# A quarter of the input loaded as fp32 on ScalarE's DMA queue, and the prologue's small work put in another order

## The chip, the cores and the metric

The kernel runs on one core of one Trainium2 chip. The metric is the device time of one execution, in microseconds. Three timed runs of the kernel before stand beside one profiled execution, from which every row in this document comes. TensorE appears in the rows as PE (its weight loads as PEld), VectorE as DVE, ScalarE as ACT, GpSimd as POOL and SyncE as SP.

## What is computed

A filter in the frequency domain along the sequence, and then a two-layer network whose activation is a PReLU:

```
X = np.fft.rfft(x, axis=1)                       # x: 8 x 3008 x 256, fp32
Y = X * (filt_r + 1j * filt_i)[None]             # 1505 frequencies x 256
y = np.fft.irfft(Y, n=3008, axis=1)
h = y.reshape(24064, 256) @ w_in                 # 256 x 2048
g = np.maximum(h, 0.0) + alpha * np.minimum(h, 0.0)
out = g @ w_out                                  # 2048 x 256, out in fp32
```

## The kernel before

The transform of 3008 = 47 x 64 points is done in stages of small matmuls: over the 47 (stage a), with twiddles over the 64 (stage b), times the filter, and the same back (stages c and d). The tokens are then taken in 47 blocks of 512 for the two matrix products. The transforms of the batches 1 to 7 are put by a table of steps (PLACES and its neighbours) among the matmuls of the blocks; that part of the program is not touched here. What is touched is the **prologue**: the transform of batch 0 (the class First), with the turning of the constant tables, before the first block can start.

**x.** One batch of x comes in four quarters, each 94 rows (two halves h of 47) by 2048 columns. A half is read as 47 rows of 8 KB. load_x (L197 to L201) issues the two halves of a quarter on GpSimd's queue; the DMA itself rounds fp32 to fp16 on its way into the tile xs.

**Tables.** c_twp holds half of the twiddle table in fp16 and lands in uw_s. turn_p(j) (L473 to L482) multiplies eight columns of it by a signed permutation on TensorE, and four evictions of 128x256 write the rest of twf_s and twa_s; for j = 1 VectorE evicts, for j = 0 and 2 ScalarE. GpSimd copies the untouched half into twf_s and twa_s (L450 to L452). turn_i (L484 to L490) transposes eight columns by 16 matmuls against the identity id16 in idx_s and evicts 128x1024 into twi_s or twx_s, the tables of stage c.

**Order.** It is written out by hand in the program: every engine takes its instructions in the order of the text, and waits are for data and buffers. The queues around the change are these:

- SP: idx_s (identity and the matrix of stage a, L446), the table (L447), alpha (L448), and later, behind waits on GpSimd's small copies, wf1_s (94 rows, L517) and other constants.
- GpSimd: eight x loads, the small identity id32, the four table copies, then the filter in pieces of four columns (load_g, four DMAs each), the first half of w_in, and from L541 on small work on alpha, which needs al_s; then the loads of batch 1 and the rest of the weights. L577 changes the sign of one block of w_in where alpha is over 1.
- TensorE: 16 warm-up matmuls on id16, turn_p(0), turn_p(1), turn_i into twi_s, turn_p(2), turn_i, and then the sixteen piece_a(i) of stage a (L341 to L349; i // 4 is the quarter of x), with the two turn_i into twx_s after i = 3 and 7, alpha's transpose at i = 6 (its eviction is al_s, L505), and four more warm-up matmuls at i = 11 and at the end. Then come turn_at (L351) and piece_b (L359), which take the result of all sixteen.
- ScalarE and VectorE evict piece_a in turns (even i ScalarE, odd i VectorE), each in a tile of 128x384.

PSUM banks go round in pairs: side(i) gives one of two banks of psF for even i and one of two accumulators of the output (wbank) for odd i; turn_i takes the wide psH.

Of the kernel before, what the change touches and what calls it, by code (L numbers as in the profile page):

```python
# [10 lines left out]
FP16 = mybir.dt.float16  # L11
FP32 = mybir.dt.float32

NFFT = 3008
N1 = 47
N2 = 64
NK1 = 24
D = 256
# [94 lines left out]
def kernel(  # L113
# [10 lines left out]
    nc = tc.nc  # L124
# [20 lines left out]
    idx_d = nc.inline_tensor(idx_np.astype(np.float16), name="c_idx")  # L145

    konst = ctx.enter_context(tc.tile_pool(name="konst", bufs=1))
    p_x = ctx.enter_context(tc.tile_pool(name="p_x", bufs=4))
# [16 lines left out]
    twi_s = konst.tile([128, NK1, 128], FP16, name="twi_s")  # L165
# [17 lines left out]
    idx_s = konst.tile([128, 224], FP16, name="idx_s")  # L183
# [5 lines left out]
    gflat = gtb.rearrange("p a b -> p (a b)")  # L189
    twx_s = tw_s.rearrange("p a k c -> p (a k) c")[:, 0:NK1]  # L190
    yT = konst.tile([128, 2, 2 * NFFT], FP16, name="yT")

    def xrow(b, h, c):
        return bass.AP(tensor=x.tensor, offset=x.offset + (b * NFFT + NH * h + 8 * c) * D,
                       ap=[[N2 * D, N1], [1, 8 * D]])

    def load_x(b, c, halves=(0, 1)):  # L197
        if 0 in halves:
            xc[(b, c)] = p_x.tile([2 * N1, 8 * D], FP16, name="xs")
        for h in halves:  # L200
            nc.gpsimd.dma_start(out=xc[(b, c)][h * N1 : h * N1 + N1], in_=xrow(b, h, c))  # L201

    def load_filt(dst, pbase, src, ka, kb):
        n = kb - ka
        nc.gpsimd.dma_start(
            out=dst[pbase : pbase + 32, ka:kb],
            in_=bass.AP(tensor=src.tensor, offset=src.offset + ka * D,
                        ap=[[47 * D, 32], [D, n], [1, D]]))
        nc.gpsimd.dma_start(
            out=dst[pbase + 32 : pbase + 64, ka:kb],  # L210
            in_=bass.AP(tensor=src.tensor, offset=src.offset + (N1 - ka) * D,
                        ap=[[47 * D, 32], [-D, n], [1, D]]))
# [5 lines left out]
    def bank(wide=False):  # L218
        if wide:
            return psH.tile([128, 2, 512], FP32, name="hps")[:, 0]  # L220
        turns[0] += 1
        return psF[turns[0] % 2].tile([128, 512], FP32, name="psF")
# [100 lines left out]
    def on_act(o, i):  # L323
        nc.scalar.activation(o, i, AF.Copy)  # L324

    def on_dve(o, i):
        nc.vector.tensor_copy(o, i)
# [102 lines left out]
    xc = {}  # L430

    def load_g(ka, kb):
        load_filt(filt_s, 0, filt_r, ka, kb)
        load_filt(filt_s, 64, filt_i, ka, kb)

    def load_w(h):
        for kt in range(2):
            nc.gpsimd.dma_start(out=win_s[:, kt, 1024 * h : 1024 * h + 1024],
                                in_=moe_w_in[kt * 128 : (kt + 1) * 128, 1024 * h : 1024 * h + 1024])

    nc.vector.memset(al_s[0:1, 0:1], 0.0)
    nc.scalar.activation(alm_s[0:1, 0:1], al_s[0:1, 0:1], AF.Copy)
    for c in range(4):
        load_x(0, c)
    make_identity(nc, id32)
    nc.sync.dma_start(out=idx_s, in_=idx_d.ap())  # L446
    nc.sync.dma_start(out=uflat[:, 0 : 128 + NK1 * 64], in_=twp_d.ap())  # L447
    nc.sync.dma_start(out=al16, in_=moe_alpha.rearrange("(j p) -> j p", p=128))  # L448
    f0 = First()
    for ka, kb in ((0, 8), (8, 24)):  # L450
        for t, o in ((twf_s, 0), (twa_s, 64)):
            nc.gpsimd.tensor_copy(t[:, ka:kb, o : o + 64], twp_s[:, ka:kb])  # L452
    load_g(0, 4)
    load_g(4, 8)

    def warm(n, pw=None):
        pw = wbank() if pw is None else pw
        for _ in range(n):
            nc.tensor.matmul(pw[:, 0:128], id16, id16, start=True, stop=True)

    def wbank():
        return obank().rearrange("p k d -> p (k d)")

    def side(i):
        return wbank() if i % 2 else bank()
# [7 lines left out]
    def turn_p(j):  # L473
        k = slice(8 * j, 8 * j + 8)
        ps = side(j)
        nc.tensor.matmul(ps, tur, twp_s[:, k].rearrange("p k c -> p (k c)"), start=True, stop=True)
        ps = ps.rearrange("p (k h c) -> p k h c", h=2, c=32)
        ev, neg = (on_dve, minus_dve) if j == 1 else (on_act, minus_act)
        neg(twf_s[:, k, 64:96], ps[:, :, 0])
        ev(twf_s[:, k, 96:128], ps[:, :, 1])  # L480
        ev(twa_s[:, k, 0:32], ps[:, :, 0])
        neg(twa_s[:, k, 32:64], ps[:, :, 1])  # L482

    def turn_i(ka, n, into, evict):  # L484
        ps = psH.tile([128, 2, 512], FP32, name="hps").rearrange("p a n -> p (a n)") if n == 8 else wbank()
        for k in range(n):
            w = twa_s[:, ka + k, 0:64] if into is twx_s else twp_s[:, ka + k]
            for o in (0, 64):
                nc.tensor.matmul(ps[o : o + 64, 128 * k : 128 * k + 128], w, id16, start=True, stop=True)
        evict(into[:, ka : ka + n].rearrange("p k c -> p (k c)"), ps[:, 0 : 128 * n])  # L490

    warm(16)
    turn_p(0)
    turn_p(1)
    turn_i(0, 8, twi_s, on_act)
    turn_p(2)
    turn_i(8, 8, twi_s, on_dve)
    for i in range(16):
        f0.piece_a(i, both[i % 2], side(i))
        if i == 3:  # L500
            turn_i(0, 8, twx_s, on_act)
        if i == 6:
            alp = wbank()
            nc.tensor.transpose(alp[:, 0:16], al16, id32)
            nc.vector.tensor_copy(al_s, alp[:, 0:16])  # L505
        if i == 7:
            turn_i(8, 8, twx_s, on_act)
        if i == 11:
            warm(4)
    warm(4)  # L510
    f0.turn_at(0, on_act)
    f0.turn_at(1, on_dve)
    f0.piece_b(0)
    f0.turn_at(2, on_act)
# [54 lines left out]
    for q in range(2):  # L569
        nc.gpsimd.dma_start(  # L570
            out=wout_s[:, 8 * q : 8 * q + 8],
            in_=moe_w_out[1024 * q : 1024 * q + 1024].rearrange("(j p) d -> p j d", p=128))
# [183 lines left out]
    def neg(ka, kb):  # L756
        nc.vector.tensor_scalar(filt_s[64:128, ka:kb], filt_s[0:64, ka:kb], -1.0, None, OP.mult)
# [9 lines left out]
    for b in range(1, NB):  # L767
        p = 94 * (b - 1)
# [116 lines left out]
```

## Time and profile before

| what | us |
|---|---|
| median of three runs | 762.28 |
| lowest and highest | 761.79 and 763.18 |
| the profiled execution | 761.45 |
| its span, first to last instruction | 759.7 |
| first piece_a starts (L345) | 8.01 |
| last quarter of x lands | 13.52 |
| first piece_b starts (L364) | 16.30 |
| first matmul of a block (L618) | 34.32 |

The span is what the trace covers; the execution's time has 1.75 us more around it. In the rows, a time in front is microseconds from the start of the span, L12 is line 12 of the kernel, and "out<-in" names the tile written and the tile read. In the DMA view, q0 software_dynamic is the queue that GpSimd issues to and q1 hardware_dynamic the one of SP; each carries packets to the same 16 DMA engines, and a share of 100% means that all 16 were busy through the stretch (overlapping packets can give more). The granted clock of TensorE is 1.00 throughout.

### The profile page before, as it was taken

To read this page: it belongs to the slowest core of one execution; us is meant where nothing else is said; L and a number is where in the kernel's file an instruction comes from. 1 tells how busy PE (TensorE), PEld (TensorE's weight loads), DVE (VectorE), ACT (ScalarE), POOL (GpSimd) and SP (SyncE) were. 2 spreads that over 40 slices of the span, in tenths; PEclk is the share of its full clock that TensorE was granted. 3 is DMA by queue.
4 is the path that set the end of the run, shared out by engine and by line. 5 is a ranking of instruction groups with operands and counts; after the bars stand their busy time and mean duration, and the time that the engine had idled before them with its cause. 6 is when DMAs were issued, how large, how long until landed. Compare 5 with 4: busy or idle time off the path is not lost.

```text
span 759.7 us, 19855 instructions
## 1 busy us (share of the span) xinstructions
PE 743.5 (98%) x7812; PEld 538.7 (71%) x7812; DVE 693.6 (91%) x1298; ACT 673.6 (89%) x1083; POOL 163.4 (22%) x236
## 2 busy tenths in 40 slices
PE   7999999999999999999999999999999999999998
PEld 5756666776687777776778777777777777777766
DVE  5787887998999998899999999999998997999994
ACT  6898999999999998999899998999989898888873
POOL 8641421232022220232022211221100221010100
PEclk9999999999999999999999999999999999999999
DMA  9995888778965597766876659865485355522122
GB/s 158 194 241 153 151 181 210 175 149 170 205 151 116 119 185 172 150 121 141 187 161 143 137 117 205 185 135 115 106 187 132 77 105 112 139 63 65 44 64 62
DMA packets 100790, 107.97 MB, mean 142 GB/s; under 512 B 10568, under 2 KB 81496, under 8 KB 100696
## 3 DMA queue, kind: packets, MB, share of 16 engines
q1 hardware_dynamic: 80136, 70.05, 35.9%
q0 software_dynamic: 20416, 36.58, 29.9%
q8 instruction: 61, 1.00, 0.6%
q14 instruction: 33, 0.27, 0.1%
q10 hardware_dynamic: 144, 0.07, 0.0%
HBM read 55.41 MB, written 46.66 MB: 134 GB/s over the span
## 4 chain that ended last, share of the span: by engine, by line
PE 89%; DMA 4%; ACT 3%; DVE 2%; POOL 1%; issue 1%; DVEq 0%; ACTq 0%; POOLq 0%
PE hps L618 40%; PE op L691 30%; PE op L669 6%; PE psF L245 3%; PE psF L317 3%; PE psF L265 2%; PE psF L292 2%; ACT gtb L634 1%; DMA win_s<-in_moe_w_in_dram 1%; DMA uw_s<-uw_s 1%; DMA xs<-in_x_dram 1%; PE op L723 1%; POOL xs L201 1%; DVE uw_s L278 0%; DVE gtb L821 0%
## 5 line engine op out<-in xcount | busy, mean ns | idle before, releaser
L618 PE MATMUL hps<-yT,win_s 128*128 128x512 f16 (+3 forms) x1600 | 447.6, 366 | 0.6 <-ACT yT L324 0.4
L634 ACT ACTIVATE gtb<-hps 128x1024 f16<-128x1024 f32 x376 | 386.0, 1028 | 50.9 <-PE hps L618 48.0
L691 PEld LDWEIGHTS <-gtb 128*128 128x128 f16 x3040 | 206.0, 98 | 100.0 <-issue 1.0
L640 DVE TENSOR_SCALAR m_s<-gtb,alm_s 128x512 f16<-128x512 f16 x705 | 213.9, 347 | 38.2 <-ACT gtb L634 34.9
L821 DVE TENSOR_TENSOR gtb<-gtb,m_s 128x2048 f16<-128x2048 f16 x188 | 228.9, 1217 | 5.7 <-ACT m_s L638 3.2
L691 PE MATMUL op<-wout_s,gtb 128*128 128x128 f16 x1824 | 153.3, 219 | 0.0
L618 PEld LDWEIGHTS <-win_s 128*128 128x128 f16 x1600 | 135.0, 98 | 25.3 <-issue 3.6
L281 POOL DMA_DIRECT2D uw_s<-uw_s x84 | 72.3, 1002 | 330.6 <-DVE uw_s L278 205.4
L691 PEld LDWEIGHTS <-ss 128*128 128x128 f16 x1216 | 83.1, 98 | 37.4
L691 PE MATMUL op<-tw_s,gtb 128*128 128x128 f16 x1216 | 105.0, 219 | 0.0
L691 PE MATMUL op<-tw_s,ss 128*128 128x128 f16 x1216 | 103.4, 219 | 0.0
L669 PE MATMUL op<-wout_s,gtb 128*128 128x256 f16 x512 | 76.9, 272 | 0.3 <-DVE osb L594 0.3
L656 POOL DMA_DIRECT2D gtb<-gtb x28 | 27.7, 990 | 207.9 <-ACT gtb L634 139.5
L669 PEld LDWEIGHTS <-gtb 128*128 128x128 f16 x512 | 49.9, 98 | 31.3
L324 ACT ACTIVATE asb<-psF 96x512 f16<-96x512 f32 x112 | 65.7, 601 | 1.9 <-PE psF L245 0.9
L324 ACT ACTIVATE yT<-psF 128x376 f16<-128x376 f32 x118 | 56.8, 494 | 5.0 <-PE psF L317 4.0
L324 ACT ACTIVATE v<-psF 128x512 f16<-128x512 f32 x88 | 52.0, 604 | 3.9 <-PE psF L292 2.9
L278 DVE TENSOR_TENSOR uw_s<-uw_s,filt 128x2048 f16<-128x2048 f16 x42 | 51.1, 1218 | 2.8 <-DMA uw_s<-uw_s 2.3
L201 POOL DMA_DIRECT2D xs<-in_x_dram x64 | 51.7, 974 | 6.3 <-DMA win_s<-in_moe_w_in_dram 2.4
L269 ACT ACTIVATE uw_s<-psF 128x512 f16<-128x512 f32 x84 | 50.1, 606 | 3.2 <-PE psF L265 2.2
L652 DVE TENSOR_TENSOR ss<-ss,gtb 128x1024 f16<-128x1024 f16 x76 | 51.9, 683 | 0.1
L650 DVE TENSOR_TENSOR ss<-gtb 128x1024 f16<-128x1024 f16 (+1 forms) x75 | 51.8, 690 | 0.0
(125 smaller groups left out, 642.9 us busy)
## 6 DMA issues: line engine op xcount, KB each, us to landing
out_dram<-osb SPq DMA_DIRECT2D x127, 128.0 KB
xs<-in_x_dram POOLq DMA_DIRECT2D x64, 188.0 KB, 5.8
a_dram<-asb SPq DMA_DIRECT2D x28, 384.0 KB
uw_s<-uw_s POOLq DMA_DIRECT2D x84, 128.0 KB, 3.4
v_dram<-v SPq DMA_DIRECT2D x112, 96.0 KB
zt<-v_dram SPq DMA_DIRECT2D x28, 384.0 KB
at<-a_dram SPq DMA_DIRECT2D x20, 384.0 KB
gtb<-gtb POOLq DMA_DIRECT2D x28, 256.0 KB, 4.0
```

The source lines that it names most:

```text
L201: nc.gpsimd.dma_start(out=xc[(b, c)][h * N1 : h * N1 + N1], in_=xrow(b, h, c))
L278: nc.vector.tensor_mul(w.rearrange("p (i d) -> p i d", d=1024)[:, 0 : iu // 2 + 1 : iu // 2], uu.unsqueeze(1).to_broadcast([128, 2, 1024]), f)
L281: nc.gpsimd.dma_start(out=uu[o : o + 64], in_=ww[64 - o : 128 - o], accum_op=OP.add)
L324: nc.scalar.activation(o, i, AF.Copy)
L618: nc.tensor.matmul(self.hps[:, j % 2, ca:cb], win_s[:, kt, j * 128 : (j + 1) * 128], yT[:, kt, at : at + cb - ca], start=(kt == 0), stop=( ...
L634: nc.scalar.activation(g, hs, AF.Copy)
L640: nc.vector.tensor_scalar(ms[:, i], g[:, i], 0.0, a, OP.min, OP.mult)
L650: nc.vector.tensor_add(z1, a21, a22)
L652: nc.vector.tensor_add(z2, z1, a11)
L669: nc.tensor.matmul(op[:, si % 2], self.pair(k // 2)[:, k % 2, 128 * si : 128 * si + 128], wout_s[:, k], start=(k == 0), stop=(k == 15))
L691: nc.tensor.matmul(acc[:, 128 * i : 128 * i + 128], x[:, k, 128 * i : 128 * i + 128], b[:, k], start=first and k + i == 0, stop=k == 7, sk ...
L821: nc.vector.tensor_add(g, g, ms)
```

## The change

The first quarter of x no longer goes through GpSimd's queue. ScalarE's own queue carries idx_s (which leaves SP's queue), and then the two halves of that quarter in fp32, unrounded, into a part of gtb that is unused until stage b; VectorE rounds it to fp16 into xs in two copies of 94x1024, ahead of everything else that it has to do but a memset. GpSimd issues the other three quarters, and its filter loads stand between the pairs of table copies instead of after all of them. On TensorE the third turn_p and the second turn_i move behind piece_a(3), the turns into twx_s behind piece_a(7) and piece_a(15), and the two warm-ups of four become one of eight; the last eviction into twx_s stands behind that of turn_at(0).

```diff
+    xf = gflat[0 : 2 * N1, 6144:10240].bitcast(FP32)
+    nc.scalar.dma_start(out=idx_s, in_=idx_d.ap())
+    for h in range(2):
+        nc.scalar.dma_start(out=xf[h * N1 : h * N1 + N1], in_=xrow(0, h, 0))
     nc.vector.memset(al_s[0:1, 0:1], 0.0)
     nc.scalar.activation(alm_s[0:1, 0:1], al_s[0:1, 0:1], AF.Copy)
-    for c in range(4):
+    xc[(0, 0)] = p_x.tile([2 * N1, 8 * D], FP16, name="xs")
+    for c in range(1, 4):
         load_x(0, c)
     make_identity(nc, id32)
-    nc.sync.dma_start(out=idx_s, in_=idx_d.ap())
     nc.sync.dma_start(out=uflat[:, 0 : 128 + NK1 * 64], in_=twp_d.ap())
     nc.sync.dma_start(out=al16, in_=moe_alpha.rearrange("(j p) -> j p", p=128))
     f0 = First()
     for ka, kb in ((0, 8), (8, 24)):
         for t, o in ((twf_s, 0), (twa_s, 64)):
             nc.gpsimd.tensor_copy(t[:, ka:kb, o : o + 64], twp_s[:, ka:kb])
-    load_g(0, 4)
-    load_g(4, 8)
+        load_g(ka // 2, ka // 2 + 4)
...
-        evict(into[:, ka : ka + n].rearrange("p k c -> p (k c)"), ps[:, 0 : 128 * n])
-
+        o, i = into[:, ka : ka + n].rearrange("p k c -> p (k c)"), ps[:, 0 : 128 * n]
+        return evict(o, i) if evict else (o, i)
+
+    for s in range(2):
+        on_dve(xc[(0, 0)][:, 1024 * s : 1024 * s + 1024], xf[:, 1024 * s : 1024 * s + 1024])
     warm(16)
     turn_p(0)
     turn_p(1)
     turn_i(0, 8, twi_s, on_act)
-    turn_p(2)
-    turn_i(8, 8, twi_s, on_dve)
     for i in range(16):
         f0.piece_a(i, both[i % 2], side(i))
         if i == 3:
-            turn_i(0, 8, twx_s, on_act)
+            turn_p(2)
+            turn_i(8, 8, twi_s, on_dve)
         if i == 6:
             alp = wbank()
             nc.tensor.transpose(alp[:, 0:16], al16, id32)
             nc.vector.tensor_copy(al_s, alp[:, 0:16])
         if i == 7:
-            turn_i(8, 8, twx_s, on_act)
+            turn_i(0, 8, twx_s, on_act)
         if i == 11:
-            warm(4)
-    warm(4)
+            warm(8, bank(True))
+    last = turn_i(8, 8, twx_s, None)
     f0.turn_at(0, on_act)
+    on_act(*last)
     f0.turn_at(1, on_dve)
```

## The prediction

> **What bounds the kernel now.** I read the page first, then the chain that ended last in order of time, then tables by stage, then the DMA view in narrow stretches.
>
> ```profile
> span 759.7 us, 19855 instructions
> PE 743.5 (98%) x7812; PEld 538.7 (71%) x7812; DVE 693.6 (91%) x1298; ACT 673.6 (89%) x1083; POOL 163.4 (22%) x236
> ```
>
> The profiled execution took 761.45 us, 1.75 us more than its span; the median of the runs shown is 762.28 us, 0.83 us above it. The steady part is TensorE's, so the prologue's time stands in the total undiluted. The tables by stage (columns: stretch, length, busy time of PE, PEld, DVE, ACT and POOL, clock, DMA share, GB/s) say so: 676.42 us of PE in the 680 us from 60 to 740, and 1.53 us of PE idle from 36 to 40.
>
> ```profile
> 1.00:2.00 1.00, 0.00 (x0) 0.00 (x0) 0.00 (x0) 1.00 (x1) 0.75 (x2) 1.00 0.18 50
> 2.00:3.00 1.00, 0.49 (x5) 0.50 (x6) 0.00 (x0) 0.21 (x2) 1.00 (x3) 1.00 0.74 154
> ...
> 36.00:40.00 4.00, 2.47 (x18) 1.18 (x16) 2.82 (x6) 3.67 (x6) 2.89 (x5) 1.00 1.07 208
> ...
> 60.00:740.00 680.00, 676.42 (x7146) 490.71 (x7145) 643.30 (x1211) 617.38 (x991) 126.08 (x161) 1.00 0.65 140
> ```
>
> The chain (start, us, what) in the prologue:
>
> ```profile
> 4.95 8.57 DMA xs<-in_x_dram
> ...
> 13.66 0.33 PE psF L345 x4
> ...
> 15.65 0.61 ACT at L324
> ...
> 39.44 1.53 POOL win_s L577
> ```
>
> The last quarter of x, issued at 4.95, lands at 13.52; the last four of the first-stage pieces follow (L345), their evictions, and the turned block at 15.65. So what the prologue waits for is x. VectorE's own order up to there:
>
> ```profile
> 5.52 0.42 DVE L471 TENSOR_SCALAR twf_s<-op 128x256 f16<-128x256 f32 x1 [4.67 <-PE op L476]
> ...
> 6.52 0.41 DVE L471 TENSOR_SCALAR ss<-op 128x256 f16<-128x256 f32 x1
> 7.64 1.23 DVE L327 CAST twi_s<-hps 128x1024 f16<-128x1024 f32 x1 [0.70 <-PE hps L489]
> 8.78 1.01 DVE L327 CAST gtb<-op 128x384 f16<-128x384 f32 x2
> 10.46 0.56 DVE L327 CAST gtb<-op 128x384 f16<-128x384 f32 x1 [0.67 <-PE op L345]
> 10.94 0.16 DVE L505 COPY al_s<-op 128x16 f32<-128x16 f32 x1
> 11.44 0.56 DVE L327 CAST gtb<-op 128x384 f16<-128x384 f32 x1 [0.34 <-PE op L345]
> 12.45 1.02 DVE L327 CAST gtb<-op 128x384 f16<-128x384 f32 x2 [0.46 <-PE op L345]
> 14.19 1.02 DVE L327 CAST gtb<-op 128x384 f16<-128x384 f32 x2 [0.72 <-PE op L345]
> ```
>
> It evicts the last piece at 15.21 (14.19 + 1.02). Everything later hangs on that moment.
>
> **The change part by part: the fp32 quarter.** Two of POOL's eight x loads go. In their place ScalarE issues two copies of 47 rows of 8 KB. First the price of such a row. The DMA view from 9 to 11 us, when POOL's x loads are all that moves:
>
> ```profile
> DMA packets 144, 0.42 MB, mean 211 GB/s; under 512 B 41, under 2 KB 41, under 8 KB 144
> ...
> q0 software_dynamic: 144, 0.42, 107.0%
> ```
>
> 103 packets are rows (the other 41 are under 512 B): 1.07 x 2 us x 16 engines / 103 = 0.33 us each, and 0.31 us apart, since the packets overlap by 1.07. Each reads 8 KB and writes 4 KB; I take 0.31 us for a row that writes 8 KB as well.
>
> Next, on how many engines. The only other copy on a hardware queue whose rows come in 47s is wf1_s, 94 rows (L517). Its stretch from 15.79 to 16.04, then, for contrast, the 128 rows of idx_s from 1.72 to 1.85:
>
> ```profile
> q0 software_dynamic: 17, 0.02, 74.3%
> q1 hardware_dynamic: 21, 0.00, 7.9%
> ```
> ```profile
> q1 hardware_dynamic: 41, 0.02, 50.6%
> ```
>
> With 94 rows waiting, the queue kept 7.9% of 16 = 1.3 engines busy; with 128 rows it kept 50.6%, 8.1 engines. So a hardware queue doesn't spread a copy over whatever is free: 94 rows ran on one or two engines. If rows go out in equal shares, 94 = 2 x 47 fits two, and **47, a prime, fits one**. This inference is the step on which the forecast stands.
>
> The Trainium skill states it as a rule (DMA: Bandwidth & Descriptors, section "Why a DMA increments its semaphore by 16 and not by 1"): a copy runs on the largest number of engines up to 16 that divides both patterns' slowest dimension, on hardware queues the lowest-numbered ones, while POOL's path may give some copies all 16. By that rule both halves share one engine; the 94 rows of wf1_s agree (1.3 engines seen in 0.25 us), and no copy of 47 rows on a hardware queue is in this trace.
>
> Both halves on one engine are 94 x 0.31 = 29.1 us of that engine. The other work that is queued on it meanwhile:
>
> ```profile
> q0 software_dynamic: 3161, 3.85, 79.6%
> q1 hardware_dynamic: 1104, 1.41, 15.8%
> ...
> xs<-in_x_dram POOLq DMA_DIRECT2D x12, 188.0 KB, 7.1
> win_s<-in_moe_w_in_dram POOLq DMA_DIRECT2D x4, 256.0 KB, 7.6
> filt<-in_filt_r_dram POOLq DMA_DIRECT2D x12, 64.0 KB, 4.3
> filt<-in_filt_i_dram POOLq DMA_DIRECT2D x12, 64.0 KB, 4.1
> ```
>
> That is the DMA view of 0 to 31 us. POOL can issue x's other three quarters, all 24 filter pieces and the first half of win_s before it must wait for al_s (L541), which now comes after x. An x load is 47 x 0.31 / 16 = 0.91 us of each engine, so six are 5.5; the filters by bytes 24 x 64 / 188 x 0.91 = 7.4; half of win_s 2.5; SP's tables 15.8% of 31 = 4.9. Together 20.3 us. If the engine takes from its queues in turn, the shorter heap is through before the fp32 rows are, and these end after the sum of both: 1.7 (first packets; share 0.18 in 1 to 2) + 29.1 + 20.3 = **51.1 us**.
>
> **VectorE's part.** The two roundings (94x1024 each) stand first in VectorE's order, so turn_p(1)'s four evictions wait behind them, and PE at L345 with all after it. No row shows this rounding. Bounds: 0.35 us (the 128x512 fp16 TENSOR_SCALAR of L640 at 347 ns) and 1.23 us (the 128x1024 CAST of 7.64, same operation, size and types, but from PSUM). I take the nearest, 1.23, so 2.46 for two.
>
> ```profile
> L640 DVE TENSOR_SCALAR m_s<-gtb,alm_s 128x512 f16<-128x512 f16 x705 | 213.9, 347 | 38.2 <-ACT gtb L634 34.9
> ```
>
> The Trainium skill (VectorE: DVE Perf Modes, section "The perf-mode tier table") gives an SBUF copy from fp32 twice the rate, 1227 ns for 2048 elements; by an estimate from its formula 0.69 us each, and the total would be 1.1 us lower.
>
> From the landing on, VectorE does 2.46 + 1.41 (turn_p(1), 5.52 to 6.93) + 1.23 (twi) + 4.17 (eight evictions: 1.01 + 0.56 + 0.56 + 1.02 + 1.02) + 0.16 = 9.4 us, now in one run, since all else has landed. It ends at 51.1 + 9.4 = 60.5 instead of 15.2: **+45.3 us**.
>
> **The rest of the edit** costs nothing beside that. ScalarE's three issues (SP's cost 0.36 and 0.41) push the table load from 0.73 to about 2 and its end to 3.3, ahead of ScalarE's first eviction at 5.09.
>
> ```profile
> 0.73 1.28 ACT L442 ACT_TABLE_LOAD   x1 [0.73 <-PEq L869]
> 0.73 0.36 SPq L446 DMA_DIRECT2D idx_s<-c_idx  x1
> ...
> 1.15 0.41 SPq L447 DMA_DIRECT2D uw_s<-c_twp  x1
> ...
> 5.09 0.38 ACT L468 ACTIVATE twf_s<-psF 128x256 f16<-128x256 f32 x1 [2.87 <-PE psF L476]
> ```
>
> idx_s on ScalarE's queue now runs beside the tables on SP's, not ahead of them; should TensorE start later than before, that is lost in its stop at L345. turn_p(2), the twi and twx turns, the longer warm-ups and POOL's table copies between filter issues move inside the 9 us in which VectorE is the bound, or inside the 40 us before; without that cover the last twx eviction, now behind turn_at(0), would cost ScalarE's 1.02 us. PE sits still for some 40 us and may restart slowly: L476's 128x512 matmul took 634 ns at 4.84, L618's 379 ns later. Behind VectorE's bound this shows only in the last turn and piece_b; up to 1 us, counted as 0 and kept in the range.
>
> ```profile
> L476 PE MATMUL op<-uw_s x1: 634/634/634, 4.8 to 4.8; 128*128 128x512 f16 x1
> ```
> ```profile
> L618 PE MATMUL hps<-yT,win_s x16: 376/379/390, 34.3 to 41.8; 128*128 128x512 f16 x16
> ```
> ```profile
> PEld L618 <- POOL win_s L577: 0.6, 1, 0.6
> ```
>
> **What comes back.** With the filters landed long before, the second block of x, win_s and wout_s find free engines, and L577 no longer holds PE (0.6 us). At most the 1.5 us of idle from 36 to 40 and a little beside it, 1.8; I take 1.0.
>
> Sum: 761.45 + 45.3 - 1.0 = 805.8 for a profiled execution, + 0.83 = 806.6, written **807 us**.
>
> **Rivals.**
> (a) One engine, but the fp32 rows hardly share it, or the halves land on two engines and share: both give 1.7 + 29.1 = 30.8. Then +25.0, **786 us**. For it: nothing here shows how an engine picks among three queues. Against: shares of 1.0 from 3 us on say that POOL's queue always has something to send.
> (b) The two copies spread over 16 engines as POOL's 47-row loads do; **not slower**. The decisive point is a landing by 15.2 - 9.4 = 5.8 us, because then VectorE isn't late. The price is 94 x 0.31 / 16 = 1.8 us of all engines, as before, and the 0.82 + 0.26 us idle in 1 to 3 are filled, at most 1.1 us gained: 761.2 to 762.3, **762 us**, which would be no change. Against it stand the 1.3 engines of wf1_s.
> (c) Spread, but landing near 7.5 since three queues share from 3 us on: VectorE is 1.7 us late, **764 us**.
> The Trainium skill (DMA: Bandwidth & Descriptors, section "Issuing engines are not separate DMA queues") says that a second issuing engine saves only issue time; that speaks for (b) or (c) staying near zero.
>
> **How the numbers follow.** Forecast 0.78, (a) 0.12, (b) 0.06, (c) 0.04. Below: (a) with roundings of 0.35 and 1.8 back, 21.5 more, 784. Above: rows at the hardware queue's own 21-to-22-us rate,
>
> ```profile
> q1 hardware_dynamic: 111, 0.20, 58.0%
> ```
>
> 0.58 x 16 us / 0.20 MB x 8192 B = 0.38, so 94 rows are 35.7, and the other heap 24.7 + 4.9 - 1.9 = 27.7 straight from the shares: 59.3 more, about 820; both at once are unlikely, so 818. The range is 784 to 818. A measurement of this kernel tells about 0.2% from no change (1.5 us). Faster by more 0.04, within 0.05, slower 0.91.
>
> **What would show it.** Right: VectorE's first rounding waits for a DMA until about 51 us, PE idle before L345, the scalar queue's rows passing at one per 0.3 to 0.6 us; then the same PE work as before, some 45 us later. Wrong: x's quarter landed before 10 us means the engine count was wrong; near 31, the sharing.

## The result and the profile after

The changed kernel takes **804.51 us** (median of five runs, 803.19 to 805.52) against 762.96 us for the kernel before, measured again with it (five runs, 761.79 to 763.32): a ratio of 1.0548, interval 1.0534 to 1.0563. It is 41.6 us slower. The profiled execution took 803.19 us.

The page of the changed kernel: the span, and the DMA queues with packets, MB and share of 16 engines.

```profile
span 801.4 us, 19866 instructions
...
q1 hardware_dynamic: 79992, 69.99, 34.3%
q0 software_dynamic: 20288, 36.20, 27.9%
...
q10 hardware_dynamic: 384, 0.89, 0.3%
```

q10 is ScalarE's queue; it had 0.07 MB before. The waits of the first 60 us (who, for whom, total, times, longest) name the cause at once:

```profile
DVE xs L327 <- DMA gtb<-in_x_dram: 45.2, 1, 45.2
ACT gtb L324 <- PE psF L345: 39.0, 3, 38.2
PEld L345 <- DVE xs L327: 38.9, 1, 38.9
...
POOL filt L209 <- DMA filt<-in_filt_r_dram: 9.3, 3, 3.6
```

VectorE waits 45.2 us for the fp32 quarter, TensorE 38.9 us for VectorE, and ScalarE for TensorE; GpSimd waits for its own earlier pieces of the filter to land. The DMA view of the changed kernel from 30 to 35 us shows the engine at work:

```profile
q0 software_dynamic: 193, 0.13, 21.2%
q10 hardware_dynamic: 13, 0.11, 5.0%
```

Thirteen rows of 8 KB pass in 5 us, and 5.0% of 16 engines is 0.8 of one engine. That fits a quarter that rides on one engine, which also serves GpSimd's queue; the experiments test it. VectorE's timeline from the landing on answers to the one shown of before:

```profile
46.07 1.29 DVE L327 CAST xs<-gtb 94x1024 f16<-94x1024 f32 x2 [45.22 <-DMA gtb<-in_x_dram]
47.28 0.41 DVE L474 TENSOR_SCALAR twf_s<-op 128x256 f16<-128x256 f32 x1
...
48.61 1.23 DVE L327 CAST gtb<-op 128x384 f16<-128x384 f32 x2
50.71 1.23 DVE L327 CAST twi_s<-hps 128x1024 f16<-128x1024 f32 x1 [0.87 <-PE hps L492]
...
52.97 0.56 DVE L327 CAST gtb<-op 128x384 f16<-128x384 f32 x1 [0.49 <-PE op L345]
54.71 1.20 DVE L327 CAST gtb<-op 128x384 f16<-128x384 f32 x2 [1.19 <-PE op L345]
56.52 1.02 DVE L327 CAST gtb<-op 128x384 f16<-128x384 f32 x2 [0.61 <-PE op L345]
```

The last first-stage eviction ends at 57.54, before it was 15.21: 42.3 us later. The stage waits for TensorE again and again, which the tables by stage explain (same columns as before; the granted clock is the figure ahead of the DMA share):

```profile
8.00:46.00 38.00, 0.13 (x4) 0.00 (x0) 0.00 (x0) 1.02 (x1) 11.32 (x22) 0.55 0.38 73
46.00:56.00 10.00, 7.90 (x91) 6.57 (x92) 7.08 (x14) 4.96 (x11) 7.19 (x16) 0.50 0.82 139
56.00:58.00 2.00, 1.95 (x42) 1.65 (x41) 1.02 (x2) 0.90 (x3) 1.89 (x4) 1.00 0.97 171
100.00:780.00 680.00, 676.48 (x7147) 490.76 (x7147) 643.17 (x1209) 618.45 (x993) 126.73 (x161) 1.00 0.65 140
```

TensorE was granted half its clock from the wait to 56 us. That figure doesn't show every slow stretch: in a second trace of the same kernel it reads 1.00 from 46 to 56 us, though the stage's matmuls took a median of 281 ns there as here (206 ns before), and in the kernel before it reads 1.00 at 4.84, where a 128x512 matmul took 634 ns against 379 later. Where the two disagree, the durations are followed here. The steady part is as it was: 676.48 us of TensorE in 680, before 676.42.

### The profile page after: what moved, and what is told of

The parts are those of the page before. It is cut to its first block, busy times and chain, and to the rows that moved or that the text cites. A ratio compares the mean times of both kernels' runs of the same rounds, so it can differ in the third digit from the quotient of the medians.

```text
span 801.4 us, 19866 instructions
## 1 busy us (share of the span) xinstructions
PE 745.7 (93%) x7812; PEld 541.5 (68%) x7812; DVE 695.1 (87%) x1300; ACT 673.9 (84%) x1083; POOL 162.3 (20%) x234
## 4 chain that ended last, share of the span: by engine, by line
PE 83%; ACT 2%; DVE 2%; DMA 1%; issue 1%; POOL 0%; DVEq 0%; ACTq 0%
PE hps L624 38%; PE op L697 29%; PE op L675 6%; PE psF L245 3%; PE psF L317 2%; PE psF L265 2%; PE psF L292 2%; DMA uw_s<-uw_s 1%; ACT gtb L640 1%; PE op L729 1%; DVE uw_s L278 0%; DVE gtb L827 0%; ACT v L324 0%; DVE m_s L646 0%; DMA v_dram<-v 0%
```

## The experiments

The theory: a copy on a hardware queue goes out in equal shares of its rows, so 47 rows use one engine and two such copies the same one; that engine's other work delays them further. The rivals: ScalarE's queue, or a row of 8 KB, is slow in itself; the sharing doesn't matter; or the new order of the small work costs. Each experiment has before-runs on its own chip beside it, to which its ratio refers.

### Rows in other numbers

The changed kernel with each half in two copies:

```diff
-        nc.scalar.dma_start(out=xf[h * N1 : h * N1 + N1], in_=xrow(0, h, 0))
+        for ra, rb in ((0, 32), (32, 47)):
+            nc.scalar.dma_start(out=xf[h * N1 + ra : h * N1 + rb], in_=bass.AP(
+                tensor=x.tensor, offset=x.offset + (ra * N2 + NH * h) * D, ap=[[N2 * D, rb - ra], [1, 8 * D]]))
```

> As the changed kernel, but each half of the fp32 quarter is issued as two copies of 32 and 15 rows, same queue, same bytes. Theory (rows go out in equal shares, so 47 rows ride on one engine): 32 rows spread over 16 engines and 15 over 15, the quarter lands at 6 to 9 us instead of 46.0, VectorE's last first-stage eviction ends at 15 to 17 us, total 761.5 to 765 us. Rival (ScalarE's queue is slow for rows of 8 KB, whatever their number): the landing stays over 30 us and the total over 790 us.

Measured 771.31 us, ratio 1.0113 (1.0098 to 1.0128). The same rows through the same queue; its DMA view from 5 to 10 us, and VectorE's timeline:

```profile
q10 hardware_dynamic: 102, 0.48, 65.2%
q0 software_dynamic: 136, 0.39, 56.2%
```
```profile
12.12 2.44 DVE L327 CAST xs<-gtb 94x1024 f16<-94x1024 f32 x2 [11.28 <-DMA gtb<-in_x_dram]
...
23.76 1.02 DVE L327 CAST gtb<-op 128x384 f16<-128x384 f32 x2 [0.64 <-PE op L345]
```

The queue now keeps 65.2% of 16, 10.4 engines busy, and VectorE's wait ends at 12.12 instead of 46.07. So neither the queue nor the row is slow; the number of rows was. The size was missed: the total is 6 us above the expected range. The landing is later than 6 to 9 us, the two roundings take 2.44 us together instead of 1.29, and the stage then runs from 14 to 24.78 as slowly as in the changed kernel. The spread alone doesn't save the idea; more on that below.

The changed kernel with the quarter in one copy of 94 rows:

```diff
-    for h in range(2):
-        nc.scalar.dma_start(out=xf[h * N1 : h * N1 + N1], in_=xrow(0, h, 0))
+    nc.scalar.dma_start(out=xf, in_=bass.AP(
+        tensor=x.tensor, offset=x.offset, ap=[[NH * D, 2], [N2 * D, N1], [1, 8 * D]]))
```

> As the changed kernel, but the fp32 quarter is one copy of 94 rows. Theory (equal shares): two engines with 47 rows each; in the changed kernel one engine had passed 45 of its rows by 20 us and 58 by 25 us, so the landing is at 20 to 23 us, and the total about 25 us below the changed kernel's, 777 to 783 us. Rival (the queue or the row size is slow): landing near 46, total near 804.

A single execution took 784.94 us, 2 us above the expected range, beside a median of 762.43 for the kernel before. Its DMA view from 15 to 20 us and VectorE's first rounding:

```profile
q10 hardware_dynamic: 24, 0.20, 9.6%
```
```profile
26.71 1.30 DVE L327 CAST xs<-gtb 94x1024 f16<-94x1024 f32 x2 [25.86 <-DMA gtb<-in_x_dram]
```

24 rows in 5 us at 9.6% of 16, 1.5 engines: two engines, each shared. The wait ends at 26.71, some 4 us past the expected landing and 19.4 before the changed kernel's. One, two and up to sixteen engines thus give 46.1, 26.7 and 12.1 us. So the number of engines sets the landing. This copy's source pattern starts with a dimension of two, the halves; whether the two engines come from that or from 94 = 2 x 47 these runs don't tell apart.

### Is it the sharing?

A GpSimd copy of one element that needs the rounded quarter stands ahead of the first filter load (the two roundings are written earlier in the program for it; their place in VectorE's order is the same):

```diff
-        load_g(ka // 2, ka // 2 + 4)
+    nc.gpsimd.tensor_copy(wf1_s[0:1, 0:1], xc[(0, 0)][0:1, 2047:2048])
+    load_g(0, 4)
+    load_g(4, 8)
```

> As the changed kernel, but a small GpSimd copy that reads the rounded quarter stands ahead of the first filter load, so that the filters, w_in and SP's later constants don't share the engine with the fp32 rows. Theory (one engine serves its queues in turn, so what else is queued on it pushes the landing back): 1.7 + 29.1 us for the rows + 5.5 for the other x loads + about 1.3 for the tables, landing at 36 to 39 us instead of 46.0; the filters then arrive as VectorE needs them, total 795 to 798 us. Rival (the landing is the pace of a lone queue and the sharing doesn't matter): landing at 45 to 46, total 804 or more.

Measured 798.89 us, ratio 1.0478 (1.0460 to 1.0496). The DMA view from 15 to 20 us, then from 20 to 25 us, and the first rounding:

```profile
q10 hardware_dynamic: 9, 0.07, 3.6%
q0 software_dynamic: 9, 0.03, 2.8%
```
```profile
q10 hardware_dynamic: 17, 0.14, 6.6%
q0 software_dynamic: 1, 0.00, 0.0%
```
```profile
40.93 1.29 DVE L327 CAST xs<-gtb 94x1024 f16<-94x1024 f32 x2 [40.09 <-DMA gtb<-in_x_dram]
```

While x's other rows are still on that engine, nine packets of each queue pass in 5 us: the engine takes from the two in turn. Once it has the fp32 rows alone, 17 pass, one in 0.29 us. The wait ends 5.1 us earlier than in the changed kernel, and by the two ratios the total is 5.3 us lower. The sharing is real, and 6.6% of 16, 1.06 engines, for the rows alone shows that both halves ride on one engine. The landing is 2 us beyond the expected range, and the total 0.9; that the first fp32 row passes at about 4 us and not at 1.7 (below) accounts for it.

### The new order alone

All four quarters through GpSimd's queue, idx_s on SP's, the rest as changed:

```diff
-    xf = gflat[0 : 2 * N1, 6144:10240].bitcast(FP32)
-    nc.scalar.dma_start(out=idx_s, in_=idx_d.ap())
-    for h in range(2):
-        nc.scalar.dma_start(out=xf[h * N1 : h * N1 + N1], in_=xrow(0, h, 0))
...
-    for c in range(1, 4):
+    for c in range(4):
         load_x(0, c)
     make_identity(nc, id32)
+    nc.sync.dma_start(out=idx_s, in_=idx_d.ap())
...
-    for s in range(2):
-        on_dve(xc[(0, 0)][:, 1024 * s : 1024 * s + 1024], xf[:, 1024 * s : 1024 * s + 1024])
```

> The other parts of the change alone: all four quarters through GpSimd's queue as before, idx_s on SP's queue, but the turns, the warm-up matmuls and the filter issues in their new order. Theory: within 0.2% of the kernel before, 761.5 to 764.5 us, because the last quarter of x still lands at 13 to 14 us and VectorE has slack. Rival (the new order costs by itself, with twi's eviction among the first-stage evictions and GpSimd's late table copies): 765 us or more.

Measured 763.88 us, ratio 1.0013 (1.0003 to 1.0023): about 1 us, inside 0.2%. And the same with twelve more matmuls on the identity ahead of the stage:

```diff
     turn_i(0, 8, twi_s, on_act)
+    warm(12, bank(True))
     for i in range(16):
```

> The new order alone, with twelve more 128x128 matmuls on the identity between the first turn into twi_s and the first first-stage piece, where TensorE sat idle for 1.2 us. Theory (the new order loses its 1.4 us because that idle time keeps the clock at half through the stage: L345's matmuls took 281 ns there against 206): L345 at 206 ns again, total 761.5 to 763 us. Rival (the order costs through its buffers and evictions): 763.5 us or more.

Measured 763.09 us, ratio 1.0013 (1.0000 to 1.0026). The first-stage matmuls of the order alone, then of the order kept busy (durations in ns, lowest, median, highest; first and last start):

```profile
L345 PE MATMUL psF<-idx_s,xs x32: 240/281/287, 7.9 to 17.0; 94*128 94x96 f16 x32
```
```profile
L345 PE MATMUL psF<-idx_s,xs x32: 202/205/216, 8.2 to 14.7; 94*128 94x96 f16 x32
```

In the profiled runs the stage was slow without the twelve and fast with them, and its last start moves from 17.0 to 14.7 us. At the first matmul of a block 1.7 us of that are left (37.15 against 35.48; before 34.32). The ratios are the same, though, so the gain in that stage is not seen in the totals, and the expectation that it gives the microsecond back is not borne out. The order by itself costs about 1 us (0.2 to 1.8 by the interval), little of the 41.6.

### The slow clock

The changed kernel with TensorE kept busy while it waits, by 610 matmuls on the identity ahead of the stage, and then by 668:

```diff
     turn_i(0, 8, twi_s, on_act)
+    warm(610, bank(True))
     for i in range(16):
```

> As the changed kernel, with 610 more 128x128 matmuls on the identity ahead of the first first-stage piece, so that TensorE is busy through most of the wait. Theory (after the wait the stage runs at half the TensorE clock, which makes 46.1 to 57.5 us out of what VectorE alone would do in about 8): the landing stays at 46, the stage's matmuls take 0.33 us a group instead of 0.50, the total falls by 1.5 to 3 us to 801.5 to 803. Rival (VectorE's order sets those 11.5 us, the clock costs nothing): total 804 to 805. If the matmuls outlast the landing, they push the total up by what they outlast it.

> As the changed kernel, with 668 more matmuls on the identity ahead of the first first-stage piece instead of 610, so that TensorE's last idle time before the landing is under 1 us instead of 3.2 us. Theory (half of TensorE's clock stretches the stage after the wait): L345's groups take 0.33 us from the first on, the stage's last eviction ends at 54 to 56 us instead of 57.5, the total is 1.5 to 3.5 us below the changed kernel, 801 to 803. Rival (VectorE's order sets the stage, the clock is not what stretches it): the matmuls are fast but the last eviction still ends at 57 and the total is 803.5 to 804.5.

Measured 803.46 us (1.0535, 1.0521 to 1.0549) and 806.02 us (1.0565, 1.0541 to 1.0590): the fall that was expected came in neither. The 610 were done 3.2 us before the landing, and the stage was slow from its first matmul, so that run tells nothing about the clock. With 668 it began fast and fell back:

```profile
46.00:50.00 4.00, 2.45 (x33) 1.63 (x33) 3.34 (x8) 1.80 (x6) 3.12 (x7) 0.83 0.65 92
50.00:54.00 4.00, 3.50 (x46) 2.98 (x43) 2.33 (x4) 1.94 (x5) 2.58 (x7) 0.50 0.94 178
```

TensorE was busy for 2.45 of the 4 us to 50, and from there the granted clock was 0.50. This run's higher total doesn't come from the prologue: the last eviction ended at 57.0 and the first block's first matmul started at 76.11, in the changed kernel at 57.5 and 76.64. It comes from the blocks, whose program is the same: from the first to the last of their matmuls on win_s they took 715.8 us against 712.9. Amid them TensorE waited 1.5 us for a DMA, and from 164.8 to 168.3 us its granted clock was 0.53.

The next kernel has the 668 as well and fills the gaps in the stage:

```diff
         f0.piece_a(i, both[i % 2], side(i))
+        if i in (2, 3, 4, 5, 6, 7, 9, 13):
+            warm(14 if i == 2 else 7, bank(True))
```

> As the changed kernel with 668 matmuls on the identity ahead of the stage, and now also 7 to 14 of them behind eight of the first-stage pieces, where TensorE waited for VectorE and its clock fell back to half. Theory (half the clock is what makes 46.1 to 57.5 us out of a stage that VectorE alone could do in about 8): L345's groups take 0.33 us through the whole stage, its last eviction ends 1.5 to 3 us after the landing's place allows, at 54 to 56 us, and the total is 801.5 to 803.5 us. Rival (the chain of banks and evictions sets the stage, whatever the clock): full clock, yet the last eviction at 57 or later and 804 us or more.

> The changed kernel itself on the same chip, as the measure for the run beside it: 803.5 to 805.5 us, the quarter landing at 45 to 47 us, the stage at half clock.

Measured 801.81 us (1.0520, 1.0501 to 1.0539) beside 804.51 us for the changed kernel on the same chip (1.0548, 1.0527 to 1.0570); their runs don't overlap (801.26 to 802.88, 803.35 to 804.93). The stage was fast to its end:

```profile
L345 PE MATMUL psF<-idx_s,xs x32: 203/206/217, 47.0 to 56.1; 94*128 94x96 f16 x32
...
L327 DVE CAST xs<-gtb x2: 681/685/689, 46.3 to 46.9; 94x1024 f16<-94x1024 f32 x2
```

The total fell by 2.7 us as expected, but the last eviction ended at 57.0, not at 54 to 56. From the first rounding to that end it is 10.8 us, against 11.8 in the run beside it; each added group holds TensorE for 0.55 to 0.95 us itself. The two profiled executions are 3.2 us apart: 1.0 is this stage, 0.5 an earlier landing (46.26 against 46.76), and with these the first block starts 1.5 us earlier (76.13 against 77.66). The other 1.7 us arise after 116 us, in the blocks. Their time varies even for one kernel, as the two traces of the changed kernel show (the last two times are the first and the last start):

```profile
L624 PE MATMUL hps<-yT,win_s x1600: 217/379/383, 76.6 to 789.5; 128*128 128x512 f16 x157, 128*128 128x384 f16 x7, 128*128 128x128 f16 x7, 128*128 128x256 f16 x7
```
```profile
L624 PE MATMUL hps<-yT,win_s x1600: 217/379/385, 77.7 to 791.3; 128*128 128x512 f16 x157, 128*128 128x384 f16 x7, 128*128 128x128 f16 x7, 128*128 128x256 f16 x7
```

They are 712.9 and 713.6 us, here it is 711.9, and 715.8 in the run with 668. So the clock costs this kernel something like 1 us in the stage; that the total fell as far as forecast is in good part luck.

### Does the idea pay once it is spread?

The kernel before, in its old order and with idx_s first on SP's queue, with the quarter as fp32 in copies of 32 and 15 rows, rounded right before the stage:

```diff
+    xf = gflat[0 : 2 * N1, 6144:10240].bitcast(FP32)
+    for h in range(2):
+        for ra, rb in ((0, 32), (32, 47)):
+            nc.scalar.dma_start(out=xf[h * N1 + ra : h * N1 + rb], in_=bass.AP(
+                tensor=x.tensor, offset=x.offset + (ra * N2 + NH * h) * D, ap=[[N2 * D, rb - ra], [1, 8 * D]]))
...
-    for c in range(4):
+    xc[(0, 0)] = p_x.tile([2 * N1, 8 * D], FP16, name="xs")
+    for c in range(1, 4):
         load_x(0, c)
...
+    for s in range(2):
+        on_dve(xc[(0, 0)][:, 1024 * s : 1024 * s + 1024], xf[:, 1024 * s : 1024 * s + 1024])
     for i in range(16):
```

> The kernel before with one thing changed: the first quarter comes as fp32 by ScalarE's queue in copies of 32 and 15 rows, and VectorE rounds it after its table evictions; idx_s stays first on SP's queue, the order of the turns is the old one. Theory (even spread over the engines the quarter lands later than through GpSimd's queue, since three queues share the same engines, and VectorE has two roundings more): landing at 9 to 11 us, last eviction at 17 to 19 us instead of 15.2, total 764 to 768 us. Rival (only the single engine and the new order were at fault, the idea itself pays, since the last quarter is issued 1 us earlier): below 762 us.

Measured 768.80 us, ratio 1.0083 (1.0067 to 1.0098). It doesn't pay. TensorE's timeline (two rows, and below them the second one's counterpart before), then VectorE's (three rows):

```profile
3.24 1.89 PE L465 MATMUL op<-idx_s 128*128 128x128 f16 x16 [3.24 <-DMA idx_s<-c_idx]
6.99 0.61 PE L482 MATMUL psF<-uw_s 128*128 128x512 f16 x1 [1.87 <-DMA uw_s<-c_twp]
```
```profile
4.44 0.61 PE L476 MATMUL psF<-uw_s 128*128 128x512 f16 x1
```
```profile
10.60 1.23 DVE L327 CAST twi_s<-hps 128x1024 f16<-128x1024 f32 x1 [1.12 <-PE hps L495]
11.74 1.29 DVE L327 CAST xs<-gtb 94x1024 f16<-94x1024 f32 x2
...
19.57 1.20 DVE L327 CAST gtb<-op 128x384 f16<-128x384 f32 x2 [0.68 <-PE op L345]
```

The rows themselves are there before VectorE asks for them (11.74, no wait). But the twiddle table, which shares the engines with them, is waited for until 6.99 instead of 4.44, everything that hangs on it moves back, and the last eviction ends at 20.8 instead of 15.2. Of these 5.6 us, 3.0 are there when VectorE evicts the first turned table (10.60 instead of 7.64), 1.3 are the two roundings behind it, and the rest arises in the stage, in which the granted clock was 0.53 from 14 to 20 us. What the early quarter gains on one queue, it takes from the tables on the other, and VectorE pays for the rounding besides. No version was found that beats the kernel before.

## Why the prediction was right, and where its sizes were off

The time was forecast at 807 and is 804.51 us, 41.6 us more than before where 44.3 was the sum. The mechanism was the forecast one, on its deciding step too: two halves of 47 rows on one engine, inferred from 94 rows that kept 1.3 engines busy. By that rule of the Trainium skill (DMA: Bandwidth & Descriptors, section "Why a DMA increments its semaphore by 16 and not by 1") 47, 94 and 32 with 15 rows give one, two and sixteen with fifteen engines; the 0.8, 1.5 and 10.4 engines that were kept busy agree.

The sum missed the profiled execution by 2.6 us (805.8 against 803.19), and two of its terms were off by more than that:

- **The landing**, 51.1 against 46.1. Two errors of opposite sign, 2.5 too little and 7.5 too much. The first fp32 row was put at 1.7 us; in the changed kernel ScalarE's queue had moved 0.07 MB by 4.2 us, which is idx_s and one row at most. The other work on that engine was put at 20.3 us; 46.1 - 4.2 - 29.1 leaves 12.8. Here GpSimd waited for earlier copies to land before it issued further ones, and these landed late (a piece of filt_r took a median of 15.9 us instead of 4.3), which their share of the slow engine explains: at 45.11 it had issued 19 of the 24 filter pieces, and w_in's first half went out at 50.28. In the run that held the filters back until the rows were through, it issued all 24 with one wait of 0.70 us. The step that failed is "POOL can issue x's other three quarters, all 24 filter pieces and the first half of win_s": it could, but not before the landing.
- **The roundings**, 2.46 us for two against 1.29. The nearest row, a CAST from PSUM, was not near. The estimate from the Trainium skill (VectorE: DVE Perf Modes, section "The perf-mode tier table") was 0.69 us each; the rows show 685 ns, so trace and page agree.
- **VectorE's run after the landing**, 9.4 us with the roundings against 11.5 (46.07 to 57.54). "Now in one run, since all else has landed" failed: VectorE waited for TensorE, whose clock was at half, for 0.87, 0.49, 1.19 and 0.61 us. The slow restart was seen and priced at nothing "behind VectorE's bound", but TensorE and the banks are in that loop. How much of it is clock alone stays between about 1 us (the filled stage) and 2.3 us (17.0 to 14.7 in the order alone).
- **What comes back**, 1.0 against 0.6: the last first-stage eviction ends 42.3 us late, the profiled execution 41.7 (803.19 - 761.45). The place was wrong. The filters had not "landed long before", as the landing shows, and the idle time from 36 to 40 did not come back: its counterpart, 78.32 to 82.32, holds the same 2.47 us of TensorE, though the DMA engines' share there is 0.37 and not 1.07. The first block still starts 42.3 us late (76.64 against 34.32); 0.2 us is won in its first 40 us, and the rest later, where two traces of one kernel differ by more.

The rows of GpSimd on which the first term rests:

```profile
45.11 0.50 POOL L205 DMA_DIRECT2D filt<-in_filt_i_dram  x1 [0.46 <-DMA filt<-in_filt_i_dram]
...
50.28 1.08 POOL L438 DMA_DIRECT2D win_s<-in_moe_w_in_dram  x2
```

Measured against the sum, the landing is 5.0 us earlier and the roundings 1.2 shorter; the rest of VectorE's run is 3.2 longer (10.2 instead of 6.9), and 0.4 less comes back. -5.0 - 1.2 + 3.2 + 0.4 = -2.6, the step from the sum's 44.3 to the profiled 41.7. That the total came so close is in part the luck of this cancelling.

Of the rivals, (a) named a real effect, as holding the filters back shows, but its 786 us needs an engine that is free from 1.7 us on. Its other reading, the halves on two engines, is not this kernel's, but the one copy of 94 rows, which had two, took 784.94. (b) and (c) fall as readings of this kernel. As prices they fall too: spread rows were put at 762 or 764 us, and the two spread kernels take 771.3 and 768.8. Two things were missing in the rivals' working: spread rows that share the engines land at 12.1 us and not at 5.8 or 7.5, as the first of the two shows, and they hold up the tables, as the second does.

## What to carry to other kernels

Before a load moves from GpSimd's queue to a hardware queue, factor its number of rows: here 47, a prime, got one engine, 94 got two, and 32 with 15 kept 10.4 busy. A small copy that is already in the trace with the same factors, like the 94 rows here, tells how many engines it will be. And where the prologue's transfers fill all engines, as they do here, look for what an early transfer on another queue holds up; here it was the table that TensorE needs first. A gain of 1 or 2 us in a prologue is read from the first block's start and not from the total alone, for the blocks of these kernels took 711.9 to 715.8 us with the same program.

## What the runs showed of the hardware that was not expected

- In this stage a fast clock didn't outlast sparse work. With TensorE busy for 2.45 of 4 us the granted clock fell from full to 0.50, though 668 matmuls had run right up to it; with the gaps filled, 3.14 of the same 4 us busy, the matmuls stayed at 206 ns. The busy share alone doesn't decide it: in the kernel before TensorE was busy for 2.47 of the 4 us from 36 to 40, and its 128x512 matmuls stayed at 376 to 390 ns. What does was not found.
- The clock can fall amid the blocks too. It did once in two of the profiled executions, with 0.53 from 164.8 to 168.3 us in the run with 668 matmuls and 0.51 from 127.0 to 130.4 in the spread quarter in the old order. The slowest 128x512 matmul took 634 ns there and 383 to 390 in the changed kernel and the one before.
- A rounding of 94x1024 took 0.68 to 0.69 us (1.29 us for two) in all the other kernels that have it. In the one with 32 and 15 rows the first, at 12.12, took 1835 ns and the second, at 13.88, 677. GpSimd's table copies ran beside the first alone, until 13.41:

```profile
11.38 1.05 POOL L458 COPY twf_s<-uw_s 128x1024 f16<-128x1024 f16 x1
12.36 1.05 POOL L458 COPY ss<-uw_s 128x1024 f16<-128x1024 f16 x1
```

That the copies are the cause was not tried.
